# Reordering the first steps of a fused FFN and spectral-filter gradient kernel, and spreading its transform units over each step

## The chip, the cores and the metric

The kernel runs on one core of one Trainium2 chip. The metric is the device time of one execution in microseconds; the time before is the median of ten executions.

## The reference

The forward pass mixes a spectral filter `a` and a gated feed-forward network `b` by a per-row gate; the kernel returns its output and the gradients of seven inputs.

```python
x = A_x  # 1 x 2048 x 576, bf16
g = sigmoid((x * gate_w).sum(-1, keepdims=True))
a = irfft2(rfft2(x) * (A_w_r + 1j * A_w_i))
b = (gelu(x @ B_w_gate) * (x @ B_w_up)) @ B_w_down    # 576 -> 4608 -> 576
out = g * a + (1 - g) * b
# and the vjp of out with grad_out: d A_x, d A_w_r, d A_w_i,
# d B_w_gate, d B_w_up, d B_w_down, d gate_w
```

The outputs `out_2`, `out_3` are the filter's gradients, `out_4` and `out_5` those of the gate and up weights (576 x 4608), `out_6` that of the down weight (4608 x 576).

## The kernel before

The 2048 rows are 16 row tiles of 128 (T), the 4608 hidden columns 18 groups of 256 (g). Phase one runs 72 steps: for each group g four steps m of four row tiles each; pr = 4 g + m numbers them, and this text calls them step 0 to step 71. Phase two (lines 1059 and on) multiplies the stored hidden tensors back to 576 columns.

**One step.** `H_mm` computes z (the gradient of the hidden product, L402 and L407, from dOT and the transposed down weight) and xy (gate and up projections, L411 for the 64 odd columns, L418 for the rest, in two halves `xy_full(0)` and `xy_full(1)`). On ScalarE (ACT) `H_da` copies z times (1 - g) to da (L430), and `H_act` copies and squares xy (L437, L439, L440). `H_ew1` makes the argument s of the gelu on VectorE (DVE; L445 to L447). `H_ew2` (called `sigs`) computes two sigmoids on ACT (L461, L462) and then eight products on DVE (L466 to L473), which end in A, dHu and dHg; it appends the three stores (L477, SP queue), which `flush` issues one step later. In the first group `sigs` of a step is held until the next step.

**W units.** The weight gradients of group g are computed while group g + 1 runs its steps: `u_dw` (L525) sums 16 row tiles for two chunks of 128 columns each into one PSUM tile `wps` (two buffers), copies it with `wevac` (L486, on ACT, or on DVE while `wcopy` says so) and stores it from POOL's queue (L531); `u_dwd` (L508) does the same for the down weight; `tail` (L538) does the 64 columns left over. `W_units` returns the list of units of each of four steps and a fifth that is carried over. The kernel has PSUM for two `wps` tiles, two `xy` tiles of two banks, and one tile of two banks with the tag `z`.

**Transform units.** The 2-D transforms of x and of grad_out, the products with the filter, and the inverse transforms are cut into units (`fwd_units`, `mid_units`, `inv_units`), each with a few matmuls into a tile of the same single slot `z`, and a copy out of it on ACT: Y (L573, L575) and ve (L588) of the forward part, Xx and Xg (L682), Vt (L769), ZT (L815), ZU (L827), ev (L844). `want` says how many units are due by each step (`FIRST` for the first eight); `fft_next` issues one. The first one of a step goes between the matmuls of `xy_full(1)`; the others go between the W units, where the weights passed so far (`at`) reach the numbers in `spots`. Vt is written to a slot of the pool `half` (two buffers) and stored by SP (L592, L771).

**Opening.** `titems` transposes four row tiles of grad_out (dB to dOT) or x (xn to xT) on TensorE (PE) in three items, whose PSUM tiles alternate between two buffers (`pgtile`) or take an xy buffer (`phtile`); each item is copied by DVE (VC) or ACT (AC). `gate(k)` computes g for four tiles (L383, L385 to L387). In the steps of group 0 the transposes of the next four tiles run between z and xy. `build_D`, `build_R` and `build_B` make the transform tables; their sines are put off to `run_late`, because ACT has to load another function table for them (1.28 us, and 1.28 back). `columns_B` makes index columns on DVE and POOL. `scale_dB` multiplies dB by (1 - g) on DVE (L946), which `u_dwd` needs.

The order on every engine is that of the program text (`manual_schedule`): nothing is moved by a scheduler.

Of the kernel before, what the change touches and what calls it, by code (L numbers as in the profile page):

```python
# [9 lines left out]
ACT = mybir.ActivationFunctionType  # L10
ALU = mybir.AluOpType
BF16 = mybir.dt.bfloat16
# [8 lines left out]
P, T = 128, 16  # L21
# [9 lines left out]
FG = 256  # L31
TPB = 512 // FG
# [212 lines left out]
def kernel(  # L245
# [12 lines left out]
    unit = Unit(ctx.enter_context(tc.tile_pool(name="unit", bufs=NUNIT, side="right")), "unit")  # L258
    hstack = ExitStack()
    hres = hstack.enter_context(tc.tile_pool(name="hres", bufs=1, side="right"))  # L260
    half = Unit(hstack.enter_context(tc.tile_pool(name="half", bufs=2, side="right")), "half")
    wpool = hstack.enter_context(tc.tile_pool(name="wpool", bufs=2, side="right"))

    wstack = ExitStack()
# [220 lines left out]
    def wevac(out, in_):  # L485
        wcopy[0](out, in_)  # L486

    def W_units(g):
        fsl = slice(g * FG, (g + 1) * FG)
        kt = kept[g]  # L490

        def tl(k, t):
            return kt[t // 4][k][:, t % 4, :]
        dwd_tiles, wp = {}, {}

        def halves(f, us):
            return [(us, lambda: f(0)), (us, lambda: f(1))]

        def wtile(key):
            if key not in wp:  # L500
                wp[key] = pw.tile([P, TPB, FG], F32, tag="wps", name="wps")
            return wp[key]

        def u_dwd(fch, h):
            def f(half):
                wps = wtile(("d", fch, h)).rearrange("p a b -> p (a b)")
                for t in range(8 * half, 8 * half + 8):
                    nc.tensor.matmul(wps[:, :288], lhsT=tl(0, t)[:, fch * P:(fch + 1) * P],  # L508
                                     rhs=dB[:, t, h * 288:(h + 1) * 288], start=(t == 0), stop=(t == T - 1))
                if half == 0:  # L510
                    return
                if h == 0:
                    dwd_tiles[fch] = stage.tile([P, D], BF16, tag="dwd", name="dwd")
                dwd = dwd_tiles[fch]
                wevac(dwd[:, h * 288:(h + 1) * 288], wps[:, :288])
                if h == 1:
                    r0 = g * FG + fch * P
                    wst[0].dma_start(out_6[r0:r0 + P, :], dwd[:])
            return halves(f, 1.0)

        def u_dw(k, ov, c0):
            def f(cc):
                wps = wtile(("w", k, c0))
                for t in range(T):
                    nc.tensor.matmul(wps[:, cc, :], lhsT=xn[:, t, (c0 + cc) * P:(c0 + cc + 1) * P],  # L525
                                     rhs=tl(k, t), start=(t == 0), stop=(t == T - 1))
                if cc == 0:
                    return
                dw = stage.tile([P, TPB, FG], BF16, tag="dw", name="dw")
                wevac(dw[:], wps[:])  # L530
                wst[0].dma_start(ov[:, c0:c0 + TPB, fsl], dw[:])  # L531
            return halves(f, 1.7)

        def tail():
            wps = wtile("t")
            for t in range(T):
                for k, r in ((1, LO), (2, HI)):
                    nc.tensor.matmul(wps[r, 0, :], lhsT=xn[:, t, 512:576], rhs=tl(k, t),  # L538
                                     start=(t == 0), stop=(t == T - 1))
            dw = stage.tile([P, FG], BF16, tag="dwt", name="dwt")  # L540
            wevac(dw[:], wps[:, 0, :])
            wst[0].dma_start(out_4[512:576, fsl], dw[LO, :])
            wst[0].dma_start(out_5[512:576, fsl], dw[HI, :])
        tl_ = [(2.0, tail)]
        w = [u_dw(k, ov, c0) for k, ov in ((1, o4v), (2, o5v)) for c0 in range(0, 4, TPB)]
        d = [u_dwd(fch, h) for fch in range(FCH) for h in range(2)]
        if g == 0:
            return [[w[0], tl_], [w[1], d[0]], d[1:], [w[2]], w[3]]
        return [[d[0]], [d[1], d[2], d[3]], [w[0], tl_], [w[1], w[2]], w[3]]


    side = []
# [323 lines left out]
    parity = iotas_R(nc, tb, res, unit)  # L876
    for f in titems(dB, dOT, 0, (pgtile, pgtile, phtile), (VC, AC, VC)):
        f()
    for f in titems(wdn, wts[0][1][:].rearrange("p k (c m) -> p k c m", c=2), 0, (phtile, pgtile, pgtile), (AC, VC, VC), n=2):
        f()  # L880
    for f in titems(xn, xT, 0, (pgtile, pgtile, pgtile), (VC, AC, VC)):
        f()
    D2[1]()
    D4[0]()
    D4[1]()
    parity()
    D4[2]()
    build_R(nc, tb, unit, 0)
    makeB = build_B(nc, tb, unit, res)

    fg = zipped(*fwd_units(xT, scr_x, None)) + zipped(*fwd_units(dOT, scr_g, gs32))
    ia, pa = inv_units(scr_p1, a_dv, SD2)
# [16 lines left out]
    mid_at = 4 * T + 10  # L909
    NPR = NT // 2  # L910
    LASTP = NG * NPR - 7
    FIRST = (0, 0, 0, 0, 0, 3, 5, 9)
    done = [0]

    def want(pr):
# [22 lines left out]

    wgT_from = 54

    carry, pend, held = [], None, []
    scaled = [0]

    def scale_dB(n):
        for t in range(scaled[0], min(scaled[0] + n, T)):
            V.tensor_scalar(dB[:, t, :], dB[:, t, :], omg32[:, t:t + 1], None, op0=ALU.mult)  # L946
            scaled[0] = t + 1

    for g in range(NG):
# [3 lines left out]
        for m in range(NPR):  # L953
# [9 lines left out]
            tiles = [ewt(tag, g) for tag in ("xb", "q", "hu")]  # L963
            state = []

            def sigs(m=m, tiles=tiles, state=state):
                H_ew2(g, m, tiles, state[0], state[1])
            if g == 0:
                pgs3 = (pgtile,) * 3
                if m < NPR - 1:  # L970
                    t1 = 4 * m + 4
                    cp = ((VC, VC, VC), (VC, VC, VC)) if m == 0 else ((VC, VC, AC), (AC, VC, VC))
                    its = titems(dB, dOT, t1, pgs3, cp[0]) + titems(xn, xT, t1, pgs3, cp[1])
                else:
                    its = []
                z, xy_full = H_mm(g, m, [lambda: gate(0)] if m == 0 else its[:2])
                da = H_da(g, m, z)
                if m > 0:
                    for f in its[2:]:
                        f()  # L980
                if held:
                    held.pop()()
                xy = xy_full(0)
                if m == 0:
                    for f in its:
                        f()
                    build_R(nc, tb, unit, 4)
                    columns_B(nc, tb, res)
                    next(makeB)
                for part in (1, 0):  # L990
                    H_act(0, xy, tiles, part)
                xy = xy_full(1)
                for part in range(2):
                    H_act(1, xy, tiles, part)
                if m < NPR - 1:
                    gate(m + 1)
                state += [H_ew1(g, tiles), da]
                if m < NPR - 1:
                    held.append(sigs)
                else:  # L1000
                    V.tensor_copy(g32[:], g_bf[:])
                    V.tensor_scalar(gs32[:], g32[:], SD2, None, op0=ALU.mult)
                    sigs()
            else:
                z, xy_full = H_mm(g, m)
                xy = xy_full(0)
                da = H_da(g, m, z)
                for part in (1, 0):
                    H_act(0, xy, tiles, part)
                xy = xy_full(1, fft_next if n else None)  # L1010
                for part in range(2):
                    H_act(1, xy, tiles, part)
                state += [H_ew1(g, tiles), da]
                if pr == 4:
                    scale_dB(12)
                elif pr == 5:
                    scale_dB(4)
                    build_R(nc, tb, unit, 8)
                    build_R(nc, tb, unit, 12)
                elif pr == 6:  # L1020
                    next(makeB)
                side_work(4.4)
                at, k = 0.0, min(n, 1)
                spots = (0.0, 1.6, 3.6) if n < 4 else (0.0, 1.0, 2.6, 4.2, 5.0, 5.0)
                tables = pr in (4, 6)
                for w, f in carry + hs:
                    if k < n and at >= spots[k - (n == 2)]:
                        fft_next()
                        k += 1
                    if tables and k == n:  # L1030
                        run_late(tb)
                        wcopy[0] = VC
                        tables = False
                    if pr == NG * NPR - 1 and at == 0.0:
                        sigs()
                    f()
                    at += w
                wcopy[0] = AC
                while k < n:
                    fft_next()  # L1040
                    k += 1
                flush()
                if pr < NG * NPR - 1:
                    sigs()
# [250 lines left out]
```

## Time and profile before

| | |
|---|---|
| median of 10 runs | 1435.67 us (1433.62 to 1438.64) |
| the profiled execution | 1435.58 us, its span 1433.8 us |
| granted TensorE clock, mean | 0.995 |
| steps 0 to 3 (9.4 to 48.3 us) | 38.85 us |
| step 4, first W units (48.3 to 68.7 us) | 20.47 us |
| steps 5 to 64 (68.7 to 887.4 us) | 818.6 us |
| phase two with the last W units (from 963 us) | 470.8 us |

The span is counted from the first instruction on the core to the last; the time is 1.8 us more. A row of the timeline gives start, duration, engine, line, operation, output<-input and shape, and in brackets how long the engine had been idle and what ended that. A row of the waits gives the engine that waited, the tile and line it waited at, who ended it, and the total in us, the number and the longest. A matmul's duration includes the drain of the array, so the distance from start to start tells what it costs: 0.107 us for 256 columns, 0.120 for 288, 0.213 for 512.

### The profile page before, as it was taken

The page shows a single profiled execution, that of the slowest core. Times are in us where ns is not written, and L with a number is a line of the kernel's source. Part 1 is how long each engine was busy: PE and PEld are TensorE (multiplying, and loading weights), DVE is VectorE, ACT ScalarE, POOL GpSimd, SP SyncE. Part 2 cuts the span into 40 slices and gives each one's busy share as a digit, 9 for nine tenths or more (in the row PEclk, how much of TensorE's full clock was granted, in tenths as well). Part 3 has the DMA queues.
Part 4 walks back from the last instruction along what each step waited for, and adds up shares of the span by engine and source line. Part 5 has one row for each costly group of instructions (what it writes and reads, how often), then busy time and mean ns, then how long its engine had stood idle before and what let it go on. Part 6 is the DMA issues. An engine that isn't in the chain of part 4 may idle for free.

```text
span 1433.8 us, 28098 instructions
## 1 busy us (share of the span) xinstructions
PE 1379.8 (96%) x11357; PEld 1026.7 (72%) x11430; DVE 736.0 (51%) x1403; ACT 731.6 (51%) x1324; POOL 223.0 (16%) x420
## 2 busy tenths in 40 slices
PE   8799999999999899999999999999999999999997
PEld 6466767766667666667767676768777777777775
DVE  7775555465888688784665657551000642112100
ACT  6777677677787788777677777662000000000000
POOL 3000000122343236330100010110000100000000
PEclk9999999999999999999999999999999999999999
DMA  7324343454564465556356554859999997788772
GB/s 213 95 83 126 96 135 105 122 139 134 134 165 127 123 163 140 144 148 156 104 156 167 130 154 131 179 127 244 206 194 203 233 189 166 159 160 173 153 150 61
DMA packets 509534, 214.62 MB, mean 150 GB/s; under 512 B 311418, under 2 KB 502588, under 8 KB 509404
## 3 DMA queue, kind: packets, MB, share of 16 engines
q1 hardware_dynamic: 493402, 187.44, 55.8%
q0 software_dynamic: 13872, 24.24, 6.0%
q8 instruction: 89, 1.46, 0.4%
q10 hardware_dynamic: 2130, 1.15, 0.3%
q14 instruction: 41, 0.34, 0.1%
HBM read 41.05 MB, written 93.84 MB: 94 GB/s over the span
## 4 chain that ended last, share of the span: by engine, by line
PE 92%; ACT 3%; DVE 2%; issue 1%; DMA 0%; POOL 0%; ACTq 0%; DVEq 0%; POOLq 0%
PE acc L1140 30%; PE wps L525 18%; PE xy L418 16%; PE wps L508 9%; PE z L402 9%; PE wps L538 2%; PE xy L411 2%; PE pf L568 2%; PE z L407 2%; PE pf L838 1%; PE pf L840 1%; PE pf L677 1%; PE pf L766 1%; PE pf L812 1%; PE pf L585 1%
## 5 line engine op out<-in xcount | busy, mean ns | idle before, releaser
L1140 PEld LDWEIGHTS <-pin 128*128 128x128 bf16 x3456 | 338.0, 98 | 85.4 <-issue 0.2
L418 PE MATMUL xy<-wgu,xT 128*128 128x512 bf16 x1079 | 256.3, 379 | 10.1 <-issue 9.4
L525 PEld LDWEIGHTS <-xn 128*128 128x128 bf16 x2304 | 225.7, 98 | 44.2 <-issue 6.1
L418 PEld LDWEIGHTS <-xT 128*128 128x128 bf16 x1152 | 106.3, 98 | 137.6 <-issue 29.9
L1157 ACT COPY bo<-acc 128x288 f32<-128x288 f32 x32 | 12.8, 399 | 304.4 <-PE acc L1140 304.4
L466 DVE TENSOR_TENSOR xb<-xb,s 128x1024 bf16<-128x1024 bf16 x72 | 49.9, 692 | 215.2 <-ACT s L462 215.2
L508 PE MATMUL wps<-dB,A 128*128 128x288 bf16 x1152 | 154.8, 286 | 1.9 <-DVE dwd L486 1.9
L402 PE MATMUL z<-wdT,dOT 128*128 128x256 bf16 x1152 | 138.5, 274 | 14.0 <-ACT ev L844 3.0
L1140 PE MATMUL acc<-wgT,pin 128*128 128x288 bf16 x1152 | 143.8, 286 | 0.0
L1140 PE MATMUL acc<-wuT,pin 128*128 128x288 bf16 x1152 | 143.6, 286 | 0.0
L1140 PE MATMUL acc<-wd_all,pin 128*128 128x288 bf16 x1152 | 142.6, 286 | 0.0
L525 PE MATMUL wps<-dHg,xn 128*128 128x256 bf16 x1152 | 136.9, 275 | 5.8 <-DVE dHg L473 5.8
L402 PEld LDWEIGHTS <-dOT 128*128 128x128 bf16 x1152 | 111.8, 98 | 33.8 <-issue 19.6
L525 PE MATMUL wps<-dHu,xn 128*128 128x256 bf16 x1152 | 135.8, 273 | 0.0
L508 PEld LDWEIGHTS <-A 128*128 128x128 bf16 x1152 | 112.0, 98 | 32.7 <-issue 2.1
L531 POOL DMA_DIRECT2D out_dram<-dw x67 | 49.3, 737 | 513.4 <-ACT dw L486 420.2
L430 ACT ACTIVATE da<-z,omg 128x256 bf16<-128x256 f32 x288 | 112.2, 471 | 12.9 <-PE z L407 12.1
L439 ACT CAST xb<-xy 128x512 bf16<-128x512 f32 x144 | 85.2, 592 | 33.7 <-PE xy L418 33.7
L1217 DVE SCALAR_TENSOR_TENSOR f32t<-gwf,dlog,b16t 128x576 f32<-128x576 f32 x16 | 13.1, 817 | 173.6 <-DMA b16t<-dxa_scr 173.6
L437 ACT ACTIVATE q<-xy 128x512 bf16<-128x512 f32 x144 | 88.1, 614 | 8.6 <-PE xy L418 6.6
L486 ACT CAST dw<-wps 128x512 bf16<-128x512 f32 x71 | 41.6, 586 | 90.9 <-PE wps L525 83.6
L440 ACT CAST hu<-xy 128x512 bf16<-128x512 f32 x144 | 87.3, 606 | 0.0
(212 smaller groups left out, 1699.0 us busy)
## 6 DMA issues: line engine op xcount, KB each, us to landing
scr<-A SPq DMA_DIRECT2D x72, 256.0 KB, 2.9
scr<-dHg SPq DMA_DIRECT2D x72, 256.0 KB, 2.9
scr<-dHu SPq DMA_DIRECT2D x72, 256.0 KB, 3.4
out_dram<-dw POOLq DMA_DIRECT2D x67, 128.0 KB, 2.3
wd_all<-in_B_w_down_dram SPq DMA_DIRECT2D x3, 1728.0 KB, 16.0
out_dram<-dwd POOLq DMA_DIRECT2D x34, 144.0 KB, 2.8
scr_p<-Vt SPq DMA_DIRECT2D x32, 145.0 KB, 2.6
wgu<-in_B_w_gate_dram SPq DMA_DIRECT2D x18, 256.0 KB, 3.9
```

The source lines that it names most:

```text
L402: nc.tensor.matmul(zo(t), lhsT=dOT[:, ci, t, :], rhs=wdT[:, ci, :], start=(t % 4 < 2 and ci == 0), stop=False)
L418: nc.tensor.matmul(xy[k][:, t % 2, :], lhsT=xT[:, ci, t, :], rhs=wgu[:, ci, :], start=False, stop=(ci == 3))
L430: nc.scalar.activation(da[:, t, :], z[:, t % 2, t // 2, :], ACT.Copy, scale=omg32[:, 4 * m + t:4 * m + t + 1])
L437: nc.scalar.activation(q[:, h, :], xy[:, :, 0:FG], ACT.Square)
L439: nc.scalar.copy(xb[:, h, :], xy[:, :, 0:FG])
L440: nc.scalar.copy(hu[:, h, :], xy[:, :, FG:2 * FG])
L466: V.tensor_tensor(xb[:], xb[:], s[:], op=ALU.mult)
L486: wcopy[0](out, in_)
L508: nc.tensor.matmul(wps[:, :288], lhsT=tl(0, t)[:, fch * P:(fch + 1) * P], rhs=dB[:, t, h * 288:(h + 1) * 288], start=(t == 0), stop=(t == ...
L525: nc.tensor.matmul(wps[:, cc, :], lhsT=xn[:, t, (c0 + cc) * P:(c0 + cc + 1) * P], rhs=tl(k, t), start=(t == 0), stop=(t == T - 1))
L531: wst[0].dma_start(ov[:, c0:c0 + TPB, fsl], dw[:])
L1140: nc.tensor.matmul(acc[:, :288], lhsT=src[:, r, :], rhs=w_of(r)[:, h * 288:(h + 1) * 288], start=(first and r == 0), stop=(last and r == F ...
```

## The change

It makes these edits:

- `u_dw` takes a `cut`: a unit consists of four parts (chunk, row tiles before or from the cut) instead of two. For group 0's first two units the cut is 12, their parts are sorted so that both chunks sum tiles 0 to 11 first, and the list of steps puts these parts in step 4 and those of tiles 12 to 15 in step 5, with the tail and one `u_dwd`.
- For all other groups the tail stands first in its step; its output takes a slot of the tag `dw` instead of one of its own.
- The pool `half` has three buffers.
- The opening's transposes of x, tables and `gate(0)` go between the two parts of z of step 0. In step 0 all transposes of tiles 4 to 7 and those of dB's tiles 8 to 11 run between the halves of xy; the later ones are also issued earlier than before. The third `wdn` item takes an xy buffer.
- `sigs` of step 3 is held and issued in step 4. `columns_B` stays in step 0, the constants of `build_B` are made in step 1.
- dB is scaled half on ACT in step 4 and half on DVE in step 5. The tables 8 and 12 and `build_B` are made in steps 6 and 7, the sines in steps 5 and 7.
- The units due in the first eight steps are 0, 0, 0, 0, 0, 0, 3, 5. The others of a step are put at equal shares of the step's weight (`total * k / n - 0.45`) instead of at `spots`.

```diff
-    half = Unit(hstack.enter_context(tc.tile_pool(name="half", bufs=2, side="right")), "half")
+    half = Unit(hstack.enter_context(tc.tile_pool(name="half", bufs=3, side="right")), "half")
...
-        def u_dw(k, ov, c0):
-            def f(cc):
+        def u_dw(k, ov, c0, cut=T // 2):
+            both = cut != T // 2
+
+            def f(cc, t0, t1):
                 wps = wtile(("w", k, c0))
-                for t in range(T):
+                for t in range(t0, t1):
...
-                if cc == 0:
+                if cc == 0 or t1 < T:
                     return
...
-            return halves(f, 1.7)
+            parts = [(cc, t0, t1) for cc in range(TPB) for t0, t1 in ((0, cut), (cut, T))]
+            if both:
+                parts.sort(key=lambda a: a[1])
+            return [(1.7 * (a[2] - a[1]) / T, lambda a=a: f(*a)) for a in parts]
...
-            dw = stage.tile([P, FG], BF16, tag="dwt", name="dwt")
+            dw = stage.tile([P, TPB, FG], BF16, tag="dw", name="dwt")
...
         if g == 0:
-            return [[w[0], tl_], [w[1], d[0]], d[1:], [w[2]], w[3]]
-        return [[d[0]], [d[1], d[2], d[3]], [w[0], tl_], [w[1], w[2]], w[3]]
+            return [[w[0][:2], w[1][:2]], [w[0][2:], w[1][2:], tl_, d[0]], d[1:], [w[2]], w[3]]
+        return [[d[0]], [d[1], d[2], d[3]], [tl_, w[0]], [w[1], w[2]], w[3]]
...
-    FIRST = (0, 0, 0, 0, 0, 3, 5, 9)
+    FIRST = (0, 0, 0, 0, 0, 0, 3, 5)
...
+                head_, early, mid_, late_ = [
+                    ([opening], [], items(dB, dOT, 1, VC, VC, VC) + items(xn, xT, 1, VC, VC, VC)
+                     + [lambda: build_R(nc, tb, unit, 4)] + items(dB, dOT, 2, AC, AC, VC), []),
+                    ([], items(xn, xT, 2, VC, VC, VC), [], items(dB, dOT, 3, AC, AC, VC)),
+                    ([], items(xn, xT, 3, VC, VC, VC), [], []),
+                    ([], [], [], [])][m]
...
-                if m < NPR - 1:
-                    held.append(sigs)
                 else:
...
-                    sigs()
...
+                state += [H_ew1(g, tiles), da]
+                held.append(sigs)
             else:
                 z, xy_full = H_mm(g, m)
                 xy = xy_full(0)
                 da = H_da(g, m, z)
+                if held:
+                    held.pop()()
...
                 if pr == 4:
-                    scale_dB(12)
+                    scale_dB(8, True)
                 elif pr == 5:
-                    scale_dB(4)
+                    scale_dB(8)
+                elif pr == 6:
                     build_R(nc, tb, unit, 8)
+                    next(makeB)
+                elif pr == 7:
                     build_R(nc, tb, unit, 12)
-                elif pr == 6:
-                    next(makeB)
                 side_work(4.4)
+                jobs = carry + hs
+                total = sum(w for w, _ in jobs)
                 at, k = 0.0, min(n, 1)
-                spots = (0.0, 1.6, 3.6) if n < 4 else (0.0, 1.0, 2.6, 4.2, 5.0, 5.0)
-                tables = pr in (4, 6)
-                for w, f in carry + hs:
-                    if k < n and at >= spots[k - (n == 2)]:
+                tables = {5: 4, 7: 1}.get(pr)
+                for i, (w, f) in enumerate(jobs):
+                    if k < n and (at >= total * k / n - 0.45 or len(jobs) - i <= n - k):
                         fft_next()
                         k += 1
-                    if tables and k == n:
+                    if i == tables:
                         run_late(tb)
                         wcopy[0] = VC
-                        tables = False
```

More of the change, by code (lines that the diff above doesn't have):

```diff
@@ L519, in u_dwd @@
             return halves(f, 1.0)
-        def u_dw(k, ov, c0):
-            def f(cc):
+        def u_dw(k, ov, c0, cut=T // 2):
+            both = cut != T // 2
+            def f(cc, t0, t1):
                 wps = wtile(("w", k, c0))
-                for t in range(T):
+                for t in range(t0, t1):
                     nc.tensor.matmul(wps[:, cc, :], lhsT=xn[:, t, (c0 + cc) * P:(c0 + cc + 1) * P],
-                                     rhs=tl(k, t), start=(t == 0), stop=(t == T - 1))
-                if cc == 0:
+                                     rhs=tl(k, t), start=(t == 0 and (cc == 0 or not both)),
+                                     stop=(t == T - 1 and (cc == 1 or not both)))
+                if cc == 0 or t1 < T:
                     return
@@ L539, in tail @@
                                      start=(t == 0), stop=(t == T - 1))
-            dw = stage.tile([P, FG], BF16, tag="dwt", name="dwt")
-            wevac(dw[:], wps[:, 0, :])
-            wst[0].dma_start(out_4[512:576, fsl], dw[LO, :])
-            wst[0].dma_start(out_5[512:576, fsl], dw[HI, :])
+            dw = stage.tile([P, TPB, FG], BF16, tag="dw", name="dwt")
+            wevac(dw[:, 0], wps[:, 0, :])
+            wst[0].dma_start(out_4[512:576, fsl], dw[LO, 0, :])
+            wst[0].dma_start(out_5[512:576, fsl], dw[HI, 0, :])
         tl_ = [(2.0, tail)]
-        w = [u_dw(k, ov, c0) for k, ov in ((1, o4v), (2, o5v)) for c0 in range(0, 4, TPB)]
+        w = [u_dw(k, ov, c0, 12 if g == 0 and k == 1 else T // 2) for k, ov in ((1, o4v), (2, o5v)) for c0 in range(0, 4, TPB)]
         d = [u_dwd(fch, h) for fch in range(FCH) for h in range(2)]
         if g == 0:
-            return [[w[0], tl_], [w[1], d[0]], d[1:], [w[2]], w[3]]
-        return [[d[0]], [d[1], d[2], d[3]], [w[0], tl_], [w[1], w[2]], w[3]]
+            return [[w[0][:2], w[1][:2]], [w[0][2:], w[1][2:], tl_, d[0]], d[1:], [w[2]], w[3]]
+        return [[d[0]], [d[1], d[2], d[3]], [tl_, w[0]], [w[1], w[2]], w[3]]
     side = []
@@ L878, with opening @@
         f()
-    for f in titems(wdn, wts[0][1][:].rearrange("p k (c m) -> p k c m", c=2), 0, (phtile, pgtile, pgtile), (AC, VC, VC), n=2):
+    for f in titems(wdn, wts[0][1][:].rearrange("p k (c m) -> p k c m", c=2), 0, (phtile, pgtile, phtile), (AC, VC, VC), n=2):
         f()
[L881 to L888, printed above, removed]
-    makeB = build_B(nc, tb, unit, res)
+    makeB = build_B(nc, tb, unit, res)
+    def opening():
+        for f in titems(xn, xT, 0, (pgtile, pgtile, pgtile), (VC, AC, VC)):
+            f()
+        D2[1]()
+        D4[0]()
+        D4[1]()
+        parity()
+        D4[2]()
+        build_R(nc, tb, unit, 0)
+        gate(0)
     fg = zipped(*fwd_units(xT, scr_x, None)) + zipped(*fwd_units(dOT, scr_g, gs32))
@@ L939, with scale_dB @@
     wgT_from = 54
-    carry, pend, held = [], None, []
+    carry, pend, held, rest = [], None, [], []
     scaled = [0]
-    def scale_dB(n):
+    def scale_dB(n, on_act=False):
         for t in range(scaled[0], min(scaled[0] + n, T)):
-            V.tensor_scalar(dB[:, t, :], dB[:, t, :], omg32[:, t:t + 1], None, op0=ALU.mult)
+            if on_act:
+                nc.scalar.activation(dB[:, t, :], dB[:, t, :], ACT.Copy, scale=omg32[:, t:t + 1])
+            else:
+                V.tensor_scalar(dB[:, t, :], dB[:, t, :], omg32[:, t:t + 1], None, op0=ALU.mult)
             scaled[0] = t + 1
@@ L964, with sigs, items @@
             state = []
-            def sigs(m=m, tiles=tiles, state=state):
+            def sigs(g=g, m=m, tiles=tiles, state=state):
                 H_ew2(g, m, tiles, state[0], state[1])
             if g == 0:
-                pgs3 = (pgtile,) * 3
-                if m < NPR - 1:
[L971 to L976, printed above, removed]
+                def items(src, dst, t, *cp):
+                    return titems(src, dst, 4 * t, (pgtile,) * 3, cp)
+                head_, early, mid_, late_ = [
[4 more added lines that the diff above has]
+                    ([], [], [], [])][m]
+                if m == 1:
+                    rest.append(late_.pop())
+                elif m == 2:
+                    head_ = [rest.pop()]
+                z, xy_full = H_mm(g, m, head_)
                 da = H_da(g, m, z)
-                if m > 0:
-                    for f in its[2:]:
-                        f()
+                for f in early:
+                    f()
                 if held:
@@ L983 @@
                 xy = xy_full(0)
+                for f in mid_:
+                    f()
                 if m == 0:
-                    for f in its:
-                        f()
-                    build_R(nc, tb, unit, 4)
                     columns_B(nc, tb, res)
+                elif m == 1:
                     next(makeB)
@@ L996 @@
                     gate(m + 1)
-                state += [H_ew1(g, tiles), da]
-                if m < NPR - 1:
-                    held.append(sigs)
                 else:
@@ L1002 @@
                     V.tensor_scalar(gs32[:], g32[:], SD2, None, op0=ALU.mult)
-                    sigs()
+                for f in late_:
+                    f()
+                state += [H_ew1(g, tiles), da]
+                held.append(sigs)
             else:
```

## The prediction

> **What bounds the kernel now.** I read the shares first, then the chain, then the waits of PE, then the places of the longest waits in order of time. Share and chain:
>
> ```profile
> PE 1379.8 (96%) x11357; PEld 1026.7 (72%) x11430; DVE 736.0 (51%) x1403; ACT 731.6 (51%) x1324; POOL 223.0 (16%) x420
> PE 92%; ACT 3%; DVE 2%; issue 1%; DMA 0%; POOL 0%; ACTq 0%; DVEq 0%; POOLq 0%
> ```
>
> PE carries the end from start to finish. The order of instructions shows that both kernels issue the same number of matmuls, so the only thing to win is time in which PE stands still (span 1433.8 less 1379.8 busy: 54.0 us) or runs at a lower clock. Who makes it stand still (total us, times, longest):
>
> ```profile
> PE wps L525 <- DVE dHg L473: 5.8, 1, 5.8
> PE z L402 <- ACT ev L844: 3.0, 4, 0.8
> PE z L402 <- ACT Vt L769: 2.9, 1, 2.9
> PE z L402 <- ACT ve L588: 2.2, 3, 0.8
> PE z L402 <- ACT ZT L815: 2.2, 2, 1.1
> PE wps L508 <- DVE dwd L486: 1.9, 1, 1.9
> PE z L402 <- ACT Y L575: 1.7, 2, 0.8
> ```
>
> Two kinds are seen. One long wait stands at the first W tile. All rows "z <- ACT ..." are one thing: the single z bank pair still holds the last transform unit of a step when the next step wants it (with the smaller rows 13.6 us in 16 waits; a further 4.3 us in 6 waits where one unit waits for another). The long wait in order of time, and the clock just after it:
>
> ```profile
> 61.87 0.69 DVE L473 TENSOR_TENSOR dHg<-hu,om 128x1024 bf16<-128x1024 bf16 x1
> 62.61 4.31 PE L525 MATMUL wps<-dHg,xn 128*128 128x256 bf16 x20 [5.76 <-DVE dHg L473]
> 62.60:66.90 4.30, 4.29 (x22) 2.80 (x23) 4.20 (x14) 4.23 (x6) 0.00 (x0) 0.53 0.70 194
> ```
>
> Twenty matmuls took 4.31 us; elsewhere sixteen of them take 1.91 us with the drain, 0.107 us from start to start. The third line (PEclk 0.53) says why: after the wait PE ran at half clock until 66.7, about 2.0 us more. The stall at step 34 is of this kind too:
>
> ```profile
> 467.82 0.81 ACT L769 CAST Vt<-pf 128x580 bf16<-128x580 f32 x1 [3.83 <-DMA scr_p<-Vt]
> 468.68 2.87 PE L402 MATMUL z<-wdT,dOT 128*128 128x256 bf16 x16 [2.92 <-ACT Vt L769]
> ```
>
> ACT could not write Vt, since both slots were still being stored; z came 3.1 us late (start to start) and sixteen matmuls took 2.87 us instead of 1.91. An everyday end of a step:
>
> ```profile
> 151.12 0.42 PE L585 MATMUL pf<-Y,Rt 128*128 128x290 bf16 x2
> ...
> 151.58 0.64 ACT L588 COPY ve<-pf 128x580 f32<-128x580 f32 x1
> ...
> 152.27 1.58 PE L402 MATMUL z<-wdT,dOT 128*128 128x256 bf16 x13 [0.73 <-ACT ve L588]
> ```
>
> The unit is the last work of its step, its copy takes 0.64 us, and z starts 0.9 us late.
>
> **A rule against the row.** The Trainium skill, "TensorE: Matmul & The Clock Gate", section "What's actually happening", lets the clock fall after an idle window of about 3.4 us. The row disagrees on the edge: 2.92 us was enough here for half clock from 469.4 to 472.9. By the rule the Vt stall is worth 3.1 us; by the row 3.1 + 1.7 = 4.8. I take the row, and charge the same to any new stall of about 3 us.
>
> **The change, part by part.**
>
> Opening (steps 0 to 3). z of step 0 moves ahead of the xn transposes; its last weight copy ends at 7.98 (ACT, 0.59 from 7.39), so z runs 8.05 to 9.8 instead of 9.40 to 11.1, and the 20 transposes and their copies follow uncovered: gate at about 12.1 instead of 11.15, a loss of 0.95. In step 0 twenty more transposes (1.3 us) come forward from step 1, with two ACT copies of 1.01; all of it is a move. What sets the pace is the loop ACT sigmoids (2.1) - DVE products (5.2, 57.28 to 62.48) - DVE s (1.05) - sigmoids: 8.6 us with its latencies, as the starts of the product chains at 40.04, 48.66 and 57.28 show. Followed by hand through the new order, these chains start at 29.1, 39.2, 47.7 and 56.5, and PE reaches the W matmuls of step 4 at about 54.5 instead of 55.4. Gain 0.9; bounds -3 to +2.
>
> First W tiles. The first 48 matmuls now need only tiles 0 to 11, whose dHg is done by 52.9: the wait of 5.9 (start to start) and its 2.0 of half clock go. What is late next: in step 5 the tail needs the PSUM slot of the first W tile, copied by ACT. ACT's queue up to there: two halves of xy of step 4 (six copies in 3.05, from 58.59) end at 59.4; eight scalings of dB, a form the trace does not have on ACT. The rule of "ScalarE: Activation LUTs", "Rules for kernel authors", is to put a multiplication on VectorE, and DVE's row agrees on price (0.287 each, 12 in 3.44). On ACT a bound from below is the 128x512 copy, 0.48 from start to start, from above the 1024 sigmoid, 1.08; in proportion to the columns 0.54, so 8 x 0.54 = 4.3 (3.8 to 8.6). By the rule's argument the move loses 8 x 0.25 = 2.0; by place about 0.9, as the sigmoids behind it must wait for DVE until 62.8 anyway. So ACT: scaled at 63.7, sigmoids to 65.8, da to 67.2, xy to 70.2, first W copy to 70.9. PE ends its sixteen matmuls of step 5 at 67.1 and waits 3.8, and by the row above loses 1.7 of clock. So 5.9 + 2.0 is exchanged for 3.8 + 1.7. Bounds of the new stall with its clock: 1 to 10.
>
> Tables. The sine loads (1.28 each) and their work move from steps 4 and 6 to 5 and 7. The wait of 2.0 at 92.9 (wps for a DVE copy held by the table work) goes. In step 7 the transform copy ve now stands behind the table work on ACT (1.28 + 0.67 + 0.49 + 0.67 = 3.1 us): z of step 8 waits about 1.8; before, steps 7 and 8 lost 0.95 twice. columns_B stays in step 0, its mask constants go to step 1: POOL idles there, nothing. The sigmoids of step 3, issued in step 4 behind da, are counted above. On SP the stores of step 3 and the weight loads of group 2 keep their order, only the Vt stores fall elsewhere between them, and SP waits there for its sources (L592 127.7 us, L477 80.5), not they for it: nothing.
>
> Sum up to step 8: gone 5.9 + 2.0 + 2.0 + 1.9, with the opening's 0.9 makes 12.7; new 3.8 + 1.7 + 1.8 = 7.3. **Gain 5.4.**
>
> Spread of the transform units. In the old order twelve times a unit has no matmul between itself and the next user of z, and the pairs behind xy have only four (0.85 us); a last unit with eight (0.96) is enough for a copy of 0.64 but not for two of 0.64 (Xg: 0.56 lost before z four times) or the 1.02 of ZT. In the new order the least cover is 0.85 everywhere. Removed after step 8: the 17.9 us of the wait rows are 21.6 from start to start; less the 1.9 already counted and 0.3 that is clock, and with the 1.7 of clock after the Vt stall: 21.1. The Vt stall is in it, removed by the third slot: the store lands after 2.6 us in the median, and three slots ask for a delay of one more unit before ACT waits.
>
> New short waits: a cover of 0.85 against need (0.64 copy + about 0.3 latency) leaves 0.05 to 0.1 at some dozen places, ZT (1.02) with 0.85 to 0.96 leaves 0.34 to 0.45 five times: 3.5 together. And a second unit now comes one W part (0.85) behind xy, where ACT first works off three copies of xy's second half (1.5): its own copy ends 2.15 behind xy. Where a third unit follows within 0.85, it waits 0.2 to 0.4; I count ten such at 0.3: 3.0. Bounds for both: 2 to 18. **Gain 21.1 - 6.5 = 14.6.**
>
> Tail first in its step and its use of the dw stage slot: its copy (0.37) and the two stores stand 3.4 us from the next copy; POOL's queue is idle there. Nothing. Four more transform units are left over for later steps (first due 5 instead of 9 by step 7): pure move, the last still falls in step 64. The last 471 us (phase two) are untouched.
>
> **Sum.** 5.4 + 14.6 = 20.0. The profiled run is 1435.58 (span 1433.8 plus 1.8 around it), the median 1435.67: the same. 1435.6 - 20 = **1415.6 us**.
>
> **Rivals.**
> - *The waits move inside the steps* (0.2). For: ACT is 72 to 79% busy in this stage, and copies queue behind xy's. Against: most units are not followed within 0.85. At 15 us of new waits the gain is 5.4 + 6 = 11.5: 1424.
> - *No early gain* (0.15). The lag of ACT at steps 5 to 8 lasts, and eats what the first W tiles won; at gain 0 there: 1421. For: ACT never idles from 56 to 72 in my chain. Against: PE has step 6's d tiles to give it room.
> - *Slower* (0.05): ACT order bounds each step. If each of the 57 steps 8 to 64 loses 0.75 (2.15 + 0.3 against 0.85 + 0.85) behind xy's copies, that is 43 us: 1435.6 - 26.5 + 43 = 1452. It decides from 26.5 / 57 = 0.47 us a step. Against: steps of two or three units put the second past the middle, 1.7 us or more behind xy.
> - *The stall stays as it was* (0.05): a tile of the first twelve is late, too, and the early part costs 4 more: 1425. The order of instructions shows that the waits are on steps 0 to 2 alone.
>
> My forecast holds 0.55. Range: bounds in gain of the opening (-3.9, +1.1), of the exchange (-4.5, +4.5), of the spread (-11.5, +4.5), not all at once: **1404 to 1429**. What a measurement can tell from no change is 0.2%, 2.9 us. Faster 0.91, same 0.04, slower 0.05.
>
> **What would show it.** Right: no wait of wps on dHg; the waits of z on ev, ve, ZT, Y and Vt together under 7 us; a wait of tail or W for an ACT copy of 3 to 4 us near 67 to 71; z of step 8 near 102. Wrong: PE waits of 0.3 or more in most steps at L568, L585, L838 or L812; W matmuls of step 4 later than 57; a half clock anywhere but near 70.

## The result and the profile after

The changed kernel takes 1412.96 us (median of 8 runs, 1411.96 to 1414.84) against 1435.92 for the kernel before (29 runs): ratio 0.9841, 95% interval 0.9832 to 0.9849, a gain of 23 us. The profiled execution spans 1410.2 us, 23.6 less than before.

Shares and chain of the kernel after, from its page:

```profile
PE 1376.2 (98%) x11357; PEld 1026.2 (73%) x11430; DVE 731.0 (52%) x1393; ACT 737.2 (52%) x1334; POOL 225.3 (16%) x420
...
PE 93%; ACT 4%; DVE 1%; issue 1%; ACTq 0%; DVEq 0%
```

PE's busy time fell by 3.6 us with the same matmuls, its idle time from 54.0 to 34.0. Of the 3.6, 2.0 are half-clock time that is gone: PE worked at half clock for 7.5 us before (62.6 to 66.7 and 469.4 to 472.9) and for 3.4 after; the rest was not traced to a cause. Who makes PE wait in the kernel after:

```profile
PE wps L544 <- ACT dw L486: 4.1, 1, 4.1
PE z L402 <- ACT ve L594: 1.6, 1, 1.6
...
PE z L402 <- ACT wdT L374: 0.9, 1, 0.9
...
PE pf L630 <- ACT RT L636: 0.5, 1, 0.5
PE pf L844 <- ACT ZT L821: 0.5, 2, 0.2
```

The rows on ev, ZT, Y, Vt, Xg and Xx in front of z are gone, and so are those on dHg and dwd. Waits of z and of transform units for ACT's copies of such units were 17.9 us in 22 places and are 2.6 in 4. In their stead stands one wait of the tail (L544) for ACT's copy of the first W tile. In order of time, ACT's queue ahead of it and the end of the wait:

```profile
59.92 5.46 ACT L956 ACTIVATE dB<-dB,omg 128x576 bf16<-128x576 bf16 x8
...
67.33 1.55 ACT L430 ACTIVATE da<-z,omg 128x256 bf16<-128x256 f32 x4
...
71.61 1.16 ACT L486 CAST dw<-wps 128x512 bf16<-128x512 f32 x2
...
72.33 0.27 PE L544 MATMUL wps<-dHg,xn 128*64 128x256 bf16 x1 [4.11 <-ACT dw L486]
```

PE had finished its W matmuls at 68.2 and stood until 72.33; ACT was never idle between 55.0 and 78.9. Busy time by stretch (PE, PEld, DVE, ACT, POOL, then granted clock, DMA share, GB/s) shows the same, and the lower clock that follows:

```profile
68.10:72.30 4.20, 0.12 (x2) 0.11 (x1) 4.10 (x8) 4.20 (x11) 0.00 (x0) 1.00 0.30 88
72.30:77.80 5.50, 5.47 (x49) 4.43 (x49) 4.46 (x13) 5.42 (x6) 2.22 (x3) 0.69 0.59 159
```

Where the 23 us came from, by the starts of z in the two traces: step 9 starts at 117.26 instead of 123.93, which is 6.7 us, less 1.9 for four transform units not yet done: 4.7. From step 9 to step 71 it is 818.4 us instead of 834.9, although those four units are done there: 18.5. Phase two: no difference (464.9 and 464.8). The stretch from step 9 to step 71 repeats from execution to execution within 0.1 us where the program is the same, so it serves below beside the ratios.

### The profile page after: what moved, and what is told of

Its sections match the earlier page's. It is cut to its first block, busy times and chain, and to the rows that moved or that the text cites. A ratio compares the mean times of both kernels' runs of the same rounds, so it can differ in the third digit from the quotient of the medians.

```text
span 1410.2 us, 28081 instructions
## 1 busy us (share of the span) xinstructions
PE 1376.2 (98%) x11357; PEld 1026.2 (73%) x11430; DVE 731.0 (52%) x1393; ACT 737.2 (52%) x1334; POOL 225.3 (16%) x420
## 3 DMA queue, kind: packets, MB, share of 16 engines
q10 hardware_dynamic: 2130, 1.15, 0.3%
## 4 chain that ended last, share of the span: by engine, by line
PE 93%; ACT 4%; DVE 1%; issue 1%; ACTq 0%; DVEq 0%
PE acc L1159 30%; PE wps L527 17%; PE xy L418 16%; PE wps L508 10%; PE z L402 9%; PE wps L544 2%; PE xy L411 2%; PE pf L574 2%; PE z L407 2%; PE pf L844 1%; PE pf L772 1%; PE pf L591 1%; PE pf L846 1%; PE pf L818 1%; PE pf L683 1%
## 5 line engine op out<-in xcount | busy, mean ns | idle before, releaser
L439 ACT CAST xb<-xy 128x512 bf16<-128x512 f32 x144 | 85.2, 592 | 23.6 <-PE xy L418 23.6
```

The lines of the kernel that those rows point to most:

```text
L439: nc.scalar.copy(xb[:, h, :], xy[:, :, 0:FG])
```

## The experiments

Each was run beside the kernel before on the same chip; ratios are against that, and the changed kernel's is 0.9841. A change of 0.001 is 1.4 us. The expected times below are on the scale of 1435.9 us for the kernel before; it took 1436.7, 1435.7 and 1433.5 on the chips of the runs, so they are compared by ratio.

**The spread of the units and what stands beside it.** First, the changed kernel with the old spots:

```diff
-                    if k < n and (at >= total * k / n - 0.45 or len(jobs) - i <= n - k):
+                    if k < n and at >= spots[min(k - (n == 2), 5)]:
```

> The changed kernel with the old spots for the transform units (all else as changed: third slot, late start of the units, first W tiles cut at twelve). Theory, the spread is the larger part: the waits of z on ve, Y, Xg, ZT and ev come back. Without the Vt stall these were 21.1 - 4.8 = 16.3 us, and the spread keeps about 1.5 of new ones, so 1413 + 15 = 1428 (1423 to 1431), and the waits of z on ACT copies are 10 us or more in the trace. Rival, the third slot and the later start did it: within 3 us of 1413.

Measured: 1423.1, ratio 0.9900 (0.9881 to 0.9918), steps 9 to 71 in 827.1 us. So the spread carries 8.7 us of the stretch. The waits for copies of transform units are 7.7 us in 14 places instead of 2.6, those of z among them 4.4 where 10 or more were expected. Both are less than forecast: something else in the change removes the other waits. Second, two Vt slots:

```diff
-    half = Unit(hstack.enter_context(tc.tile_pool(name="half", bufs=3, side="right")), "half")
+    half = Unit(hstack.enter_context(tc.tile_pool(name="half", bufs=2, side="right")), "half")
```

> The changed kernel with two Vt slots instead of three. Theory: the one long Vt wait before came from one store landing late at the very end of a step; with the units spread, a second slot is free in time, 1413 to 1415. Rival, the third slot is worth the whole stall with its clock: 1413 + 4.8 = 1418, with a wait of PE on Vt of 2 us or more and a half clock behind it.

Measured: 0.9841 (0.9823 to 0.9858), stretch 818.4: nothing. Third, the kernel before with three slots (and the tail's output in the tag `dw`, which makes room):

> The kernel before with a third Vt slot (and the tail's output in the shared slot that makes room for it), nothing else. If the stall at step 34 stands in most executions: 1435.9 - 4.8 = 1431 and no half clock near 470. If it is a late store of this one execution: 1434 to 1437.

Measured: 0.9968 (0.9956 to 0.9981), 4.6 us; stretch 830.2 instead of 834.9, and no half clock near 470. The stall is in the old order as such and not an accident of one execution, and the third slot cures it there. In the new order it had nothing left to cure. Fourth, the kernel before with equal shares:

```diff
-                spots = (0.0, 1.6, 3.6) if n < 4 else (0.0, 1.0, 2.6, 4.2, 5.0, 5.0)
...
-                    if k < n and at >= spots[k - (n == 2)]:
+                    if k < n and (at >= total * k / n - 0.45 or len(jobs) - i <= n - k):
```

> The kernel before with the equal shares for the transform units instead of the spots, nothing else. Theory: 16.3 us of waits go, about 1.5 of new ones come, the opening, the first W stall (5.9 + 2.0) and the wait at 92.9 stay: 1435.9 - 15 = 1421 (1418 to 1425). If the waits only move into the steps (rival): above 1428.

Measured: 0.9889 (0.9865 to 0.9914), 15.9 us, stretch 820.6. Of the Vt stall 1.9 us remain, without a half clock. The spread alone takes most of what the old waits cost.

**The tail's place.** The old spots cost 8.7 in the changed kernel, though the spread saves 14.4 of the stretch in the kernel before. The tail in front of the W unit was the suspect:

```diff
-        return [[d[0]], [d[1], d[2], d[3]], [tl_, w[0]], [w[1], w[2]], w[3]]
+        return [[d[0]], [d[1], d[2], d[3]], [w[0], tl_], [w[1], w[2]], w[3]]
```

> The changed kernel with the old spots and the tail behind the first W unit in its step, as before. With the old spots alone it was 1423.1, 10 us over the changed kernel where 15 were expected. If the tail's place made the other 5 (it fills the time behind xy's copies, and the W unit stands at the end): 1428. If the later start of the units made them: 1423.

Measured: 1431.0, ratio 0.9984 (0.9975 to 0.9993), stretch 838.2: 11.1 us more than with the tail first, where 5 were expected. Some of the longest waits of PE in this kernel:

```profile
PE z L402 <- ACT Xg L688: 2.8, 2, 1.4
PE z L402 <- ACT ev L850: 2.3, 3, 0.8
PE z L402 <- ACT Xx L688: 2.2, 3, 1.4
```

and one of them in order of time:

```profile
370.82 0.42 PE L683 MATMUL pf<-Vp,Btab 128*128 128x289 bf16 x2
370.93 0.37 ACT L486 CAST dwt<-wps 128x256 bf16<-128x256 f32 x1 [1.29 <-PE wps L544]
...
371.28 1.29 ACT L688 CAST Xg<-pf 64x578 bf16<-64x578 f32 x2
...
372.62 1.58 PE L402 MATMUL z<-wdT,dOT 128*128 128x256 bf16 x13 [1.37 <-ACT Xg L688]
```

The tail is a single part of weight 2.0. Where it stands last, a spot that falls due inside it takes effect behind it, with nothing left of the step, and its copy stands before the unit's on ACT. So tail first and equal shares cure the same kind of wait, and their gains do not add: 11.1 with the old spots, but 14.4 by the shares with the tail last. The 11.1 hold in this company only. Past step 9 this kernel differs from the kernel before with three slots in just two things, the four-part W units and the later start of the transform units, and its stretch is 8.0 longer (838.2 for 830.2). The four units not yet done account for 1.9 of that; the other 6.1 are a cost of these two edits under the old spots, which no run separates.

**Steps 4 to 8.** Without the cut at twelve tiles:

```diff
-            return [[w[0][:2], w[1][:2]], [w[0][2:], w[1][2:], tl_, d[0]], d[1:], [w[2]], w[3]]
+            return [[w[0]], [w[1], tl_, d[0]], d[1:], [w[2]], w[3]]
```

> The changed kernel without the cut: the first W unit sums all sixteen tiles in step 4, the second and the tail follow in step 5. Theory, exchange: the wait on dHg of about 6 with 2.0 of half clock comes back, and the wait of the tail for ACT's copy (4.1 + 1.7) goes because PE comes later: 1413 + 2.4 = 1415.4 (1414 to 1417). Rival, the cut is worth its whole wait: 1413 + 8 = 1421.

Measured: 0.9865 (0.9851 to 0.9878), 3.4 us more than the changed kernel. The wait on dHg is back (6.0) and the tail's is gone. The cut is worth about 3 us, not the 8 of the wait it removes. The sines one job later (`tables = {5: 4, 7: 2}`):

> The changed kernel with the table sines of step 7 one job later, so that the copy ve of that step stands ahead of them on ACT. Theory: the wait of 1.6 of z at 103.7 goes: 1411.4, no wait of z on ve in the trace. Rival, the sines then hold the sigmoids and da, and the same wait comes at xy: 1413.

Measured: 0.9839 (0.9825 to 0.9852): nothing. z no longer waits for ve, but the first unit of step 8 waits 1.7 for da: the rival. All scalings on DVE (`scale_dB(8)` in step 4 too):

> The changed kernel with all sixteen scalings of dB on DVE (eight in step 4, eight in step 5). By the chain: ACT's sigmoids of step 4 then wait for DVE's s (63.6) instead of the scalings (65.3), the tail starts at 70.7 instead of 72.3: -1.5, 1411.5, and up to -3.2 if the shorter wait leaves the clock alone. By price alone (0.67 on ACT as traced against 0.29 on DVE, eight times): -3.0. If DVE's products are held instead: 1413 or more.

Measured: 1411.0, 0.9825 (0.9811 to 0.9838); the tail's wait is 2.6 instead of 4.1, the half clock behind it stays, and step 71 starts 0.9 earlier (934.7 for 935.6). In this execution z of step 0 began 0.5 later (8.61 for 8.07, in the first loads), so the order itself gains 1.5, as expected. By the ratio the gain is not clear of noise: the interval overlaps that of the changed kernel, though all five times (1410.5 to 1412.0) lie under those of the kernel with the sines one job later on the same chip (1412.6 to 1413.3). Eight scalings on POOL (`nc.gpsimd.tensor_scalar` in the place of ACT's instruction):

> The changed kernel with the eight scalings that ACT does in step 4 on POOL, which idles there; the other eight stay on DVE. By the chain: ACT's sigmoids as with DVE alone, tail at 70.7 or earlier: 1409.5 to 1411.5. If POOL and DVE slow each other or POOL takes more than 3 us for one, d of step 5 waits: 1413 or more.

Measured: 0.9851 (0.9837 to 0.9864): no gain. The tail's wait shrinks to 2.5 as with DVE, but a new one of 2.3 us for a DVE copy stands in the opening. The timeline of POOL and DVE there:

```profile
29.13 14.92 POOL L956 TENSOR_SCALAR dB<-dB,omg 128x576 bf16<-128x576 bf16 x8
...
32.21 0.68 DVE L469 TENSOR_TENSOR A<-xb,hu 128x1024 bf16<-128x1024 bf16 x1
...
33.41 1.15 DVE L471 TENSOR_TENSOR om<-om,s 128x1024 bf16<-128x1024 bf16 x1
...
36.23 0.80 DVE L445 TENSOR_SCALAR s<-q 128x1024 bf16<-128x1024 bf16 x1
...
44.73 0.68 DVE L471 TENSOR_TENSOR om<-om,s 128x1024 bf16<-128x1024 bf16 x1
...
46.66 0.42 DVE L445 TENSOR_SCALAR s<-q 128x1024 bf16<-128x1024 bf16 x1
```

POOL's earlier work was done, so it ran the scalings from 29.1 to 44.1, 1.87 us each, ahead of step 4 and beside the product chains of steps 0 and 1. While it runs, some of DVE's products take up to 1.15 us and L445 0.80; the same lines take 0.68 and 0.42 once it has ended. The new wait (36.9 to 39.3) has a half clock behind it, from 39.75 for 3.41 us, and step 4 starts 3.8 later (51.71). Scalings on POOL in step 4 itself were not run.

**Towards a better version.** The x transposes ahead of z again:

```diff
+                if m == 0:
+                    for f in titems(xn, xT, 0, (pgtile, pgtile, pgtile), (VC, AC, VC)):
+                        f()
                 z, xy_full = H_mm(g, m, head_)
```

> The changed kernel with the x transposes of the opening ahead of z again, as before (the gate, the tables and the wdn item stay where the change put them). By the prediction's opening: the uncovered copies in front of the gate (0.55 at 11.4) and the late start of z fall out, -0.95: 1412.0. If the chain of sigmoids and products sets the pace anyway: 1413.0, with the W matmuls of step 4 at 55.0 as now.

Measured: 0.9840 (0.9825 to 0.9854). Step 4 starts 0.99 earlier (46.94 for 47.93) and step 6 at 77.83 as ever (77.79): the tail starts 1.0 earlier, but in this execution the clock stays at half for 6.83 us instead of 3.41 (PE works in 5.6 of them), which takes it back. That need not come of the new order: three kernels whose first six steps are those of the changed kernel (old spots, two slots, tail last) had 6.83 too. DVE scaling with the first W copies ahead of xy's on ACT:

```diff
+                if pr == 5:
+                    xy1 = xy_full(1)
+                    for _, f in hs[:4]:
+                        f()
+                    hs = hs[4:]
                 for part in (1, 0):
                     H_act(0, xy, tiles, part)
-                xy = xy_full(1, fft_next if n else None)
+                xy = xy1 if pr == 5 else xy_full(1, fft_next if n else None)
...
-                    scale_dB(8, True)
-                elif pr == 5:
-                    scale_dB(8)
+                    scale_dB(16)
...
-                tables = {5: 4, 7: 1}.get(pr)
+                tables = {5: 0, 7: 1}.get(pr)
```

(The last line keeps the sines at their place in the shortened list.)

> The changed kernel with all scalings on DVE in step 4, and in step 5 the W matmuls and their ACT copies issued ahead of ACT's copies of xy. The tail's wait (4.1, 2.6 with DVE scaling alone) and its half clock go, since the copy then runs right behind da at 67.7: tail at 68.6. Theory, ACT is the bound of steps 4 to 6: its queue (tables, sigmoids) ends at about 78 as before, so PE waits about 2 for da at the first unit of step 6, and of 4.5 us about 2.3 stay: 1411.0 - 2.3 = 1408.7. If PE bounds there: 1406.5. If all is given back: 1411.

Measured: 0.9832 (0.9818 to 0.9845). The tail no longer waits, and step 6 starts at 71.94 instead of 77.79; but the longest wait of PE in this kernel is now

```profile
PE pf L574 <- ACT da L430: 2.8, 1, 2.8
```

with a half clock behind it, and step 8 starts at 102.15. Counted from z of step 0 that is 1.6 earlier than in the changed kernel, and only 0.1 earlier than with DVE scaling alone. So the ratio, 1.3 us under the changed kernel's where 4.3 were expected, is the case "all is given back". ACT comes late to that da, and its queue began with a wait for DVE:

```profile
63.60 1.06 ACT L461 ACTIVATE om<-s 128x1024 bf16<-128x1024 bf16 x1 [3.57 <-DVE s L446]
```

From 63.6 until that da at 78.5 it idles for 0.7 us at most at a time, and two table loads of 1.28 us each are among its work. Both together:

> The last kernel with the x transposes ahead of z too. Theory: the sum of both, 1408.7 - 0.95 = 1407.8; if the chain of sigmoids sets the pace of the opening: 1408.7.

Measured: ratio 0.9820 (0.9806 to 0.9833), step 71 at 933.5 instead of 935.6. The median, 1407.8, equals the expected figure by accident, as the chip was a faster one (the kernel before took 1433.5): by ratio the gain over the changed kernel is 3.0 us, not 5.2. It is the lowest ratio of all; the two intervals meet at 0.9832 and 0.9833, so that it beats the kernel before is clear, and that it beats the changed one is likely.

## Why the prediction was right

- **PE idle is all there is to win**: held. Idle fell by 20.0 us and PE's busy time by 3.6, together the whole 23.6 of the span, with the same number of matmuls.
- **Opening.** Product chains were put at 29.1, 39.2, 47.7 and 56.5 and started at 29.4, 39.7, 48.3 and 57.2; W at 54.5 and came at 55.0. Gain 0.4 instead of 0.9. That moving z costs 0.95 held (0.99).
- **First W tiles exchanged for a wait of the tail.** Put at 67.1 to 70.9, it was from 68.2 to 72.3: 4.3 from start to start instead of 3.8. The scaling on ACT took 0.67 each, inside its bounds, instead of 0.54. The half clock came for 3.41 us, worth the 1.7 stated, but that was luck: of five executions with the same first six steps, two had 3.41 us of it and three 6.83, and in these step 6 starts 0.6 to 1.0 later, counted from z of step 0. The exchange was shown by taking the cut away: 3.4 us measured for it, where the prediction's terms give 2.4.
- **Tables.** The wait of dwd went. z of step 8 waited 1.6, 1.7 from start to start, for 1.8; it came at 103.7, while "near 102" had been named as the sign.
- **Sum up to step 8**: 4.7 for 5.4.
- **Spread.** All the waits counted in the 21.1 us are gone; the 6.5 of new ones were the mis-sized term. With the 21.1 taken as they stand, the stretch leaves 21.1 - 18.5 = 2.6 for them. So the spread gained 3.9 more than forecast and the first steps 0.7 less: 23 us for 20. The ten waits of 0.3 behind xy's copies did not appear as waits of that size: past step 9 PE lost more than 0.35 at three places only (0.67 at L630, 0.39 twice behind ZT). ZT's five places were right in kind, at 0.29 to 0.39 instead of 0.34 to 0.45.
- **Tail first costs and gains nothing**: not shown for this change, as the tail last with all else changed was not run. With the old spots it is worth 11.1 us; the prediction saw its cost and not that it keeps a unit from the end of a step. The sum came out because it counted the removed waits as one lump, whichever edit removes them.
- **Third slot**: the sum counted 4.8 for it inside the spread. That size holds for the kernel before (4.6); in the changed one the spread had done it already.
- **Rivals.** The waits did not move into the steps, ACT does not bound each step, and the early gain was not eaten. At steps 4 to 8 ACT does hold PE up: the sines one job later and the W copies first only moved the wait to da.

## What to carry to other kernels

When one buffer is shared by small units and by the head of a step, look at what stands between its uses: putting matmuls behind the last unit saved 14.4 us in the kernel before, an extra buffer 4.6. Two edits that cure the same wait do not add. The third slot was worth 4.6 us added alone and nothing when taken away, so runs of both kinds are needed to tell what an edit carries. A stall that is removed early is exchanged for the next engine's queue: follow that queue to the next wait before counting the gain.

## What the runs showed of the hardware

The clock of PE fell after shorter waits than the idle window of about 3.4 us that the Trainium skill states ("TensorE: Matmul & The Clock Gate", "What's actually happening"): after 2.3 us (scaling on POOL), 2.6 (on DVE), 2.8 (W first) and 4.1. The length of the wait alone does not decide. In steps 0 to 3 the kernel before and the same with three slots run the same program, and PE waits 1.69 us in both (from 34.0 and 34.2), but only the second lost its clock. PE's busy time is the first figure behind the comma, the granted clock the third from the end; two stretches of the kernel before, then two of the one with three slots:

```profile
32.54:35.96 3.42, 1.73 (x25) 1.20 (x23) 3.28 (x7) 1.57 (x4) 0.00 (x0) 1.00 0.54 158
35.96:39.37 3.41, 2.50 (x28) 1.72 (x27) 1.41 (x3) 2.97 (x4) 0.00 (x0) 1.00 0.13 38
...
33.29:36.70 3.41, 1.50 (x19) 0.92 (x18) 3.00 (x6) 2.00 (x5) 0.00 (x0) 1.00 0.49 142
36.70:40.11 3.41, 2.94 (x22) 2.17 (x21) 1.11 (x2) 2.94 (x4) 0.00 (x0) 0.50 0.06 19
```

The times at which the clock changes explain the choice of stretches. In the trace before they are 5.24, 59.85, 66.68, 469.45 and 472.86 us: 16, 2, 118 and 1 times 3.413 apart, and the other traces show such multiples too. Cut into windows on this grid, the fourteen traces have 18 falls, not counting the last one of each, at the very end. In 16 of them PE was busy for 1.4 us or less of the window that ended in the fall, in two for 1.5; no window with 1.68 or more ended in one, and one with 1.47 (at the Vt wait of 1.9 in the kernel before with equal shares) did not. So in these runs it was the share of a wait that fell into one window that counted, and the same wait could be free or cost 1.7 us or more.

After the tail's wait of 4.1 the clock stayed at half for 3.41 or 6.83 us, which decided up to 1 us. POOL at work beside DVE went with products of DVE up to 1.7 times as long (1.15 for 0.68), so the early place at which POOL ran the scaling was not free.
